# A fused attention and MLP block on one core: VectorE's score units moved to the projection banks, projections ordered by need, LN1 scaling on one engine

## The chip, the core and the metric

The kernel runs on 1 core of a Trainium2 chip. The engines of that core work side by side: TensorE (PE in the profile; PEld is its weight load), VectorE (DVE), ScalarE (ACT), GpSimd (POOL) and SyncE (SP), which here only issues DMAs. The metric is the device time of one execution in microseconds; the number given for a kernel is the median of its runs.

## The reference

One block with adaptive layer norm, on a sequence of S = 2048 tokens of width D = 640, with H = 32 heads of 20 and an MLP of width 1536. All inputs are bf16.

```
mod = silu(c) @ w_mod                      # six vectors of 640: sa, ca, ga, sb, cb, gb
h = layernorm(x) * (1 + ca) + sa
q, k, v = h @ wqkv, split in 32 heads of 20
p = softmax(q @ k.T / sqrt(20))            # 32 heads, 2048 x 2048 each
x = x + ga * ((p @ v) @ wo)
h = layernorm(x) * (1 + cb) + sb
x = x + gb * (((h @ w_gate) * (h @ w_up)) @ w_down)
```

## The kernel before

**Tiling.** Heads go in sets of four (index j, 8 sets). One set fills TensorE by tiling: scores use four row tiles of 32 rows (head s of the set at rows 32s), PV uses four column tiles. Queries go in five chunks (CHUNKS, L351): three of 512, two of 256. An *item* is one chunk and one set; there are 40, taken chunk by chunk. A *unit* is one PSUM bank of scores: one head, 128 keys by 512 queries, or two key tiles by 256 queries. Each item has 64 units in the chunks of 512 and 32 in the others.

**Two ways to take the exponential.** ScalarE takes most units: it reads two or three neighbouring banks in one instruction (L999) and writes bf16 probabilities to a ring PP of 8 slots. VectorE takes the rest, four units (a *quad*) at a time: each unit is turned into a 16-bit integer that is read as a bf16 power of two (DB0, L1026), then the quad is shifted by five constants (DSS, L1039), and PV sums all six versions (L1364). QUADS (L352) gives the quads of an item: 2, 3, 3, 1, 1 by chunk, so 320 VectorE units and 1728 ScalarE units.

**Banks.** PSUM has 8 banks. Bank 7 gathers PV. Score groups go in turn to set A (banks 0 to 2) and set B (banks 3 and 4). In chunks 1 and 2 (WIDE) set B takes bank 5 as well. A VectorE unit sits in one bank of a group of three beside two ScalarE units (L844 to L860), and the group's set becomes free when both engines have read it. What is left, pool G (banks 5 and 6, or 6 alone), serves every *round*: an accumulation of TensorE in one bank with its evacuation (class Round, L610), for LN1 transposes (hT), K, Q and V projections, modulation columns, attention output (op), LN2 transposes, gate, up and down.

**Order.** The program of every engine is a fixed list, made by a planner in Python (class Sched, L94) with assumed durations. Each engine takes the ready task of lowest priority number. TensorE (pick_pe, L1476) takes the next score group if its set is free, then PV units in batches, then a step of a round (pick_x, L1448), then filler matmuls that keep its clock up. Rounds can carry a gate: the score group from which on they may start. `late` (L923 to L939) gives gates to the K, Q and V rounds so that they spread over chunk 0; `suffix` (L1129) does the same for op, LN2 and MLP of a chunk over the stretch of the next chunk, up to the fraction GATE_F.

**The head.** Loads of x, w_mod and the weights are issued from SP's and ScalarE's queues (L548 to L587). c is loaded transposed, one element to a partition (L548), for silu (L602 to L605). LN1 (ln1, L684) has two statistics instructions a tile on VectorE, the power -1/2 on GpSimd, and the scaling xn (L701): on VectorE for token blocks 0 and 1, on GpSimd for blocks 2 and 3 (XN_POOL). Its transposes are evacuated to hT (L721) on VectorE, two in five on ScalarE (HT_ACT). Once all projections are done, the down weights are loaded over hT's place (L946) and multiplied by gb on GpSimd (L949).

**The tail.** The last chunk's op, LN2 and MLP have no exponentials beside them. Its x is loaded (L1150) once the chunk before has written its output, whose buffer it takes.

Of the kernel before, what the change touches and what calls it, by code (L numbers as in the profile page):

```python
# [12 lines left out]
SEM = 60.0  # L13
# [4 lines left out]
DMA_RATE = 260.0  # L18
# [75 lines left out]
class Sched:  # L94

    def __init__(self):
        self.tasks = []
        self.order = {k: [] for k in ("sp", "act", "pe", "dve", "pool")}
        self.all = []
        self.free_at = {k: 0.0 for k in self.order}  # L100
        self.pend = {k: [] for k in self.order}
        self.readyl = {k: [] for k in self.order}
        self.t = 0.0
        self.n = 0
        self.progress = 0
# [9 lines left out]
        self.nfill = 0  # L115
        self.hist = []
        self.left = 0
# [31 lines left out]
    def activity(self, t, area):  # L149
        self.roll(t)  # L150
        self.ham_act += area
        self.hist.append((t, area))

# [198 lines left out]
QUADS = [2, 3, 3, 1, 1]  # L352
# [21 lines left out]
def build_kernel(nc, A_x, A_wqkv, A_wo, B_x, B_w_gate, B_w_up, B_w_down, c, w_mod, out):  # L374
# [61 lines left out]
    zfill = alloc("zfill", [128, 512], BF16)  # L436
    mhalf = alloc("mhalf", [128, 4], F32)
    warm = alloc("warm", [128, 1], F32)
    qcol = alloc("qcol", [128, 1], F32)
    csb = alloc("csb", [128, KD], BF16)  # L440
# [23 lines left out]
    for (_, n) in CHUNKS:  # L464
# [20 lines left out]
    WKQ = 2 * D + 32  # L485
    r_size = max(KD * S * 2 + KD * WKQ * 2 + KD * D * 2,
                 FT * D * 2 + FT * 512 * 2 + KD * 512 * 2 + 2 * 4 * D * 2 + 2 * KD * 128 * 2)
    r_off = region(r_size)
    R1 = Sub(r_off, r_size)
    hT = R1.alloc("hT", [128, KD, S], BF16)  # L490
    wkq = R1.alloc("wkq", [128, KD, WKQ], BF16)
    wV = R1.alloc("wV", [128, KD, D], BF16)
    R2 = Sub(r_off, r_size)
    wd_sb = R2.alloc("wd", [128, FT, D], BF16)
# [44 lines left out]
    cv = c.rearrange("o (k p) -> p (o k)", p=128)  # L539
# [8 lines left out]
    def load_c(e):  # L548
        with nc.allow_non_contiguous_dma(reason="tiny transposed c load"):
            return e.dma_start(csb[:, :], cv[:, :])  # L550

    d_c = dma("act", 4096, load_c, prio=0, dur=550.0)
# [23 lines left out]
    load_w(d_wk, 0, 1, wkq, 0, "sp", 2)  # L576
    load_w(d_wq, 0, 0, wkq, D, "act", 2)
# [7 lines left out]
    load_w(d_wk, 1, 1, wkq, 0, "sp", 5.3)  # L585
    load_w(d_wq, 1, 0, wkq, D, "sp", 5.2)
# [6 lines left out]
    p_on = pool(2400, lambda e: e.memset(Vf[:, :].rearrange("p (h w) -> p h w", w=VW)[:, :, 0:1], 1.0), prio=2)  # L593
    d_pz = dve(500, lambda e: e.memset(ps[:, BPV, :], 0.0), prio=0)
    d_zf = dve(200, lambda e: e.memset(zfill[:], 1.0), prio=0.5)
    d_wz = dve(100, lambda e: e.memset(wkq[:, :, 2 * D:WKQ], 0.0), prio=0)
# [5 lines left out]
    a_ex = act(300, lambda e: e.activation(ex[:], csb[:], AFT.Exp, scale=-1.0), [d_c], prio=5)  # L602
    d_e1 = dve(70, lambda e: e.tensor_scalar(ex1[:], ex[:], 1.0, None, op0=ALU.add), [a_ex], prio=0)
    d_rc = dve(70, lambda e: e.reciprocal(rc[:], ex1[:]), [d_e1], prio=0)
    d_sc = dve(70, lambda e: e.tensor_tensor(scol[:], rc[:], csb[:], ALU.mult), [d_rc], prio=0)  # L605
    d_SC = dve(420, lambda e: e.tensor_copy(SCb[:], scol[:].unsqueeze(2).to_broadcast([128, KD, 128])), [d_sc], prio=8)

    follower = {}

    class Round:  # L610
        def __init__(self, mms, deps, after, prio, gate=0, name=""):
# [24 lines left out]
            prev = self.evac[-1].on_start  # L636

            def rel(task):
                if prev is not None:
                    prev(task)  # L640
                G.done(b["b"], task)
            self.evac[-1].on_start = rel
# [12 lines left out]
    def col_round(v, slot, prio, plus):  # L655
# [15 lines left out]
        return r  # L671

# [37 lines left out]
    def hT_rounds(tc, prio):  # L710
# [3 lines left out]
        for k in range(KD):  # L714
# [6 lines left out]
            def after(r, k=k):  # L721
                dst = hT[:, k, tc * 512:(tc + 1) * 512]
# [14 lines left out]
    proj_last = []  # L737

    def w_deps(kind, j):
        if kind == "K":  # L740
            return [d_wk[(80 * j) // 320]] + ([d_wk[1]] if j == 3 else []) + ([d_wq[0], d_wz] if j == 7 else [])
        return [d_wq[(80 * j) // 320]] + ([d_wq[1]] if j == 3 else []) + [d_wz]

    def kq_round(kind, j, tc, prio, gate=0):
        w0 = 80 * j + (0 if kind == "K" else D)
        mms = []
        for k in range(KD):
            f = [lambda e, b, k=k, s=s: e.matmul(  # L748
                ps[32 * s:32 * s + 32, b, :], wkq[:, k, w0 + DH * s:w0 + DH * s + 32], hT[:, k, tc * 512:(tc + 1) * 512],
# [26 lines left out]
        proj_last.append(r.last)  # L776

    def v_round(t, ch, prio, gate=0):
        mms = []
        for k in range(KD):  # L780
            f = quarters(320, lambda k=k: hT[:, k, t * 128:(t + 1) * 128],
# [3 lines left out]
        def after(r):  # L785
            f = lambda e: e.tensor_copy(
                Vf[:, (t * H + 16 * ch) * VW:(t * H + 16 * ch + 16) * VW].rearrange("p (h w) -> p h w", w=VW)[:, :, 1:VW],
                ps[:, r.b["b"], 0:320].rearrange("p (h w) -> p h w", w=DH))
            return [dve(ps_cost(320), f, [r.last, p_on], prio=1)]
        r = Round(mms, list(t_hT[t // 4]) + [d_wv[ch]], after, prio, gate=gate, name=f"V{t}.{ch}")  # L790
        v_ready[(t, ch)] = r.evac[0]
        proj_last.append(r.last)

# [8 lines left out]
    class Unit:  # L802
        __slots__ = ("item", "ci", "j", "s", "kts", "n", "task", "pslot", "off", "pv_ready", "is_d", "quad", "grp", "first")
# [36 lines left out]
    ap, dp = 0, 0  # L840
    quad_left = []
    while ap < NA or dp < len(dlist):
        even = len(glist) % 2 == 0
        wide = 3 if even or ap >= NA or ubuf[ap].ci in WIDE else 2  # L844
        us = ubuf[ap:ap + wide]
        d = None
        if not quad_left and dp < len(dlist):
            quad_left = dlist[dp:dp + 4]
        if wide == 3 and quad_left and due[dp] <= ap:
            two = ubuf[ap:ap + 2]  # L850
            for u in quad_left:
                if u.s not in [v.s for v in two]:
                    d, us = u, two
                    break
        if d is not None:
            d.first = len(quad_left) == 4
            quad_left.remove(d)
            dp += 1
        ap += len(us)
        glist.append((us, d, 0 if even else 3, wide))  # L860
# [6 lines left out]
    widen, narrow = set(), set()  # L867
    bw = 2
    for g in range(1, NG, 2):
        w = glist[g][3]  # L870
        if w > bw:
            widen.add(g)
        if w < bw:
            narrow.add(g)
        bw = w

    for tc in range(4):
        ln1(tc, 2.0 + tc)
        hT_rounds(tc, 10 + 20 * tc)
# [6 lines left out]
    r_sb = col_round(3, 2, 78, False)  # L886
    r_cb = col_round(4, 3, 79, True)
# [33 lines left out]
    def g0(item):  # L921
        return max(0, int(gi * item))
    late = []  # L923
    for j in range(1, NSET):
        late.append((j - 1.2, 2560, lambda p, g, j=j: kq_round("Q", j, 0, p, g)))
        for tc in range(4):
            late.append((j - 1.15 + .2 * tc, 2560, lambda p, g, j=j, tc=tc: kq_round("K", j, tc, p, g)))
    for t in range(NT):
        late.append((0.7 + 2.6 * t / NT, 1600, lambda p, g, t=t: v_round(t, 1, p, g)))
    ql = [(tc, j) for tc in range(1, 4) for j in range(NSET)]  # L930
    for i, (tc, j) in enumerate(ql):
        late.append((3.0 + 4.7 * i / len(ql), 2560, lambda p, g, j=j, tc=tc: kq_round("Q", j, tc, p, g)))
# [3 lines left out]
    for i, (dl, w, f) in enumerate(late):  # L936
        even = NSET * acc / tot
        f(100 + i, g0(max(0.0, min(dl, even))))
        acc += w  # L939

# [35 lines left out]
    for g, (us, du, b0, wide) in enumerate(glist):  # L976
# [3 lines left out]
        allu = us + ([du] if du is not None else [])  # L980
        for i, u in enumerate(allu):
# [3 lines left out]
        ts.acq = [(bset, "b", 1 if du is None else 2)]  # L985
        if g in widen:
            ts.acq.append((G, "g5", 1, 5))
        if g in narrow:
            lastw = [act_of[g - 2]] + [d_state[glist[g - 2][1].quad[0]]["p1"][glist[g - 2][1].quad[1]]
                                       for _ in range(1) if glist[g - 2][1] is not None]  # L990
            ts.on_start = lambda task, lastw=lastw: G.add(5, lastw)
        sc.left += 1
        ts.seq = -1
        score_q.append((ts, allu))
# [22 lines left out]
        if du is not None:  # L1017
            qi, x = du.quad
            st_ = d_state[qi]
            if du.first:  # L1020
                ts.acq.append((sB0, "b0", NSH))
                assert ts.on_start is None
                ts.on_start = lambda task, st_=st_: st_.__setitem__("slot", task.slots["b0"])

            def fp1(e, st_=st_, x=x, b=b0 + nu):
                return e.tensor_scalar(DB0[:, st_["slot"], x * 512:(x + 1) * 512], bank(b), EBIAS, 0.0,  # L1026
                                       op0=ALU.add, op1=ALU.max)
            tp = Task("dve", ps_cost(512), fp1, [ts], prio=0.8, name=f"P1.{qi}.{x}")
            tp.on_start = lambda task, bset=bset: bset.done(0, task)
            sc.add(tp)  # L1030
# [98 lines left out]
    def suffix(ci):  # L1129
# [18 lines left out]
        def pr():  # L1148
            return pbase + rc_[0]
        d_xc = dma("sp", 128 * ntl * D * 2, lambda e: e.dma_start(xck[:, 0:ntl, :], xv[:, t0:t0 + ntl, :]),  # L1150
                   out_prev + proj_last, prio=15, gate=max(0, gb - 20))
# [3 lines left out]
        for tl in range(ntl):  # L1155
# [17 lines left out]
            for hf in range(2):  # L1173
                bn.append(dve(ps_cost(320), lambda e, tl=tl, hf=hf: e.bn_stats(  # L1174
                    st2[:, tl, 6 * hf:6 * hf + 6], xck[:, tl, 320 * hf:320 * hf + 320]), [ev[hf]], prio=2.8))
# [425 lines left out]
```

## Time and profile before

| what | value |
|---|---|
| median of 3 runs | 927.5 us (925.35 to 927.86) |
| profiled execution | 926.16 us, with a span of 924.3 us from the first to the last instruction |
| busy in the span | PE 858.5 us, ACT 815.4 us, DVE 729.0 us, POOL 77.8 us |
| mean granted TensorE clock | 0.978 of full speed |

The profile is of one execution. Its page has the busy time of each engine, slices of the span with the busy share of each engine in tenths, and the costliest groups of instructions; a group's row has its line, engine and operation, what it writes and reads, its count, its busy time in us and the mean of one in ns, then the idle time of the engine just ahead of it and what ended that. Busy time counts overlapping neighbours once. Matmuls are pipelined, so a busy PE is not PE at its peak. In a timeline a row begins with its start and length in us, and square brackets give the idle time ahead of it.

### The profile page before, as it was taken

The page shows a single profiled execution, that of the slowest core. Times are in us where ns is not written, and L with a number is a line of the kernel's source. Part 1 is how long each engine was busy: PE and PEld are TensorE (multiplying, and loading weights), DVE is VectorE, ACT ScalarE, POOL GpSimd, SP SyncE. Part 2 cuts the span into 40 slices and gives each one's busy share as a digit, 9 for nine tenths or more (in the row PEclk, how much of TensorE's full clock was granted, in tenths as well). Part 3 has the DMA queues.
Part 4 walks back from the last instruction along what each step waited for, and adds up shares of the span by engine and source line. Part 5 has one row for each costly group of instructions (what it writes and reads, how often), then busy time and mean ns, then how long its engine had stood idle before and what let it go on. Part 6 is the DMA issues. An engine that isn't in the chain of part 4 may idle for free.

```text
span 924.3 us, 31230 instructions
## 1 busy us (share of the span) xinstructions
PE 858.5 (93%) x13925; PEld 336.2 (36%) x13938; DVE 729.0 (79%) x1333; ACT 815.4 (88%) x774; POOL 77.8 (8%) x97
## 2 busy tenths in 40 slices
PE   5769999999997889999989799999999999999968
PEld 2324333323221322323333223333344445445547
DVE  6747877777779999989889989989777866687743
ACT  1636999999997999999999999999999999999911
POOL 3823000000006300000000000000010000000000
PEclk7979999999998999999999999999999999999989
DMA  9320000000024002210030012200301225415100
GB/s 294 106 73 2 6 5 6 5 6 4 5 54 110 6 19 48 49 33 5 30 81 5 5 42 51 48 6 20 91 8 39 64 64 111 106 29 111 43 24 18
DMA packets 101197, 42.31 MB, mean 46 GB/s; under 512 B 81864, under 2 KB 101064, under 8 KB 101064
## 3 DMA queue, kind: packets, MB, share of 16 engines
q1 hardware_dynamic: 98552, 38.44, 16.7%
q8 instruction: 110, 1.80, 0.8%
q10 hardware_dynamic: 2512, 1.89, 0.7%
q14 instruction: 23, 0.19, 0.1%
HBM read 35.06 MB, written 2.62 MB: 41 GB/s over the span
## 4 chain that ended last, share of the span: by engine, by line
PE 64%; DVE 18%; ACT 10%; POOL 4%; issue 2%; DMA 2%; SPq 1%; POOLq 0%; ACTq 0%; DVEq 0%
PE ps_all L646 19%; PE ps_all L961 18%; PE ps_all L1364 17%; ACT PP L999 10%; PE ps_all L748 8%; DVE DSS L1039 6%; DVE DB L1026 5%; POOL xn L701 2%; DMA x<-in_A_x_dram 1%; DVE xck L1165 1%; DVE st L1174 1%; DMA xck<-in_A_x_dram 1%; SPq L1110 1%; DVE h2T L1196 1%; DVE OT L1091 1%
## 5 line engine op out<-in xcount | busy, mean ns | idle before, releaser
L999 ACT ACTIVATE PP<-ps_all 128x1024 bf16<-128x1024 f32 (+1 forms) x751 | 803.9, 1167 | 53.5 <-PE ps_all L961 48.3
L961 PE MATMUL ps_all<-QT,KT 32*128 32x512 bf16 (+1 forms) x2560 | 296.5, 341 | 17.9 <-ACT PP L999 11.5
L1039 DVE TENSOR_SCALAR DSS<-DB 128x2048 int16<-128x2048 int16 x400 | 274.1, 702 | 19.9 <-PE ps_all L1364 17.9
L1026 DVE TENSOR_SCALAR DB<-ps_all 128x512 int16<-128x512 f32 x320 | 216.3, 681 | 39.2 <-PE ps_all L961 37.5
L961 PEld LDWEIGHTS ps_all<-QT,KT 32*128 32x128 bf16 x2560 | 77.3, 91 | 265.8 <-ACT PP L999 181.5
L1364 PE MATMUL ps_all<-PP,Vf 128*32 128x512 bf16 (+3 forms) x2176 | 164.2, 344 | 0.4 <-DVE OT L1091 0.2
L1364 PE MATMUL ps_all<-DSS,Vf 128*32 128x512 bf16 (+3 forms) x1920 | 145.0, 346 | 6.1 <-DVE DSS L1039 5.9
L646 PE MATMUL ps_all<-h2T,stg 128*32 128x512 bf16 (+1 forms) x1960 | 127.3, 354 | 1.9 <-DVE gsb L1236 1.0
L748 PE MATMUL ps_all<-hT,wkq 128*32 128x512 bf16 x1280 | 93.2, 389 | 0.5 <-ACT hT L724 0.5
L1364 PEld LDWEIGHTS ps_all<-PP,Vf 128*32 128x32 bf16 (+1 forms) x2176 | 48.0, 94 | 78.8 <-issue 71.8
L646 PE MATMUL ps_all<-wd,hprod 128*32 128x320 bf16 x1536 | 69.7, 301 | 0.7 <-DVE hprod L1246 0.5
L1364 PEld LDWEIGHTS ps_all<-DSS,Vf 128*32 128x32 bf16 (+1 forms) x1920 | 51.9, 96 | 33.4 <-DVE DSS L1039 14.2
L646 PEld LDWEIGHTS ps_all<-h2T,stg 128*32 128x32 bf16 x1960 | 41.9, 95 | 49.0 <-issue 24.1
L1177 POOL TENSOR_SCALAR sd<-mv 128x1 f32<-128x1 f32 x16 | 4.9, 308 | 573.5 <-DVE mv L1176 573.5
L1246 DVE TENSOR_TENSOR hprod<-ps_all,gsb 128x512 bf16<-128x512 f32 (+1 forms) x60 | 34.7, 579 | 20.9 <-PE ps_all L646 20.7
L646 PEld LDWEIGHTS ps_all<-wd,hprod 128*32 128x32 bf16 x1536 | 36.1, 96 | 25.7 <-issue 11.8
L748 PEld LDWEIGHTS ps_all<-hT,wkq 128*32 128x32 bf16 x1280 | 27.1, 97 | 38.4 <-issue 21.4
L646 PE MATMUL ps_all<-wo,Ocp 128*32 128x320 bf16 x640 | 33.5, 316 | 5.7 <-DMA xck<-in_A_x_dram 4.4
L949 POOL TENSOR_TENSOR wd<-wd,gab 128x640 bf16<-128x640 bf16 x12 | 20.4, 1738 | 200.6 <-DMA wd<-in_B_w_down_dram 200.6
L761 DVE TENSOR_SCALAR QT<-ps_all,qcol 128x512 bf16<-128x512 f32 (+1 forms) x40 | 24.9, 638 | 14.4 <-PE ps_all L748 14.4
L1091 DVE STREAM_TRANSPOSE OT<-ps_all 128x512 f32<-128x512 f32 (+1 forms) x40 | 24.2, 604 | 14.7 <-PE ps_all L1364 14.7
L1364 PE MATMUL ps_all<-DB,Vf 128*32 128x512 bf16 (+3 forms) x384 | 33.7, 347 | 1.3 <-DVE OT L1091 1.0
(62 smaller groups left out, 449.9 us busy)
## 6 DMA issues: line engine op xcount, KB each, us to landing
stg<-in_B_w_gate_dram SPq DMA_DIRECT2D x49, 160.0 KB, 2.5
stg<-in_B_w_up_dram SPq DMA_DIRECT2D x49, 160.0 KB, 2.8
out_dram<-xck SPq DMA_DIRECT2D x16, 160.0 KB
wm<-in_w_mod_dram SPq DMA_DIRECT2D x3, 800.0 KB
x<-in_A_x_dram SPq DMA_DIRECT2D x6, 320.0 KB
xck<-in_A_x_dram SPq DMA_DIRECT2D x3, 640.0 KB
wd<-in_B_w_down_dram SPq DMA_DIRECT2D x1, 1920.0 KB
stx<-in_B_w_gate_dram SPq DMA_DIRECT2D x11, 160.0 KB
```

The costliest lines, as they stand in the source:

```text
L646: return lambda e, b: e.matmul(ps[32 * x:32 * x + 32, b, 0:n], lhs()[:, 32 * x:32 * x + 32], rhs(), tile_position=(0, 32 * x), start=st, s ...
L701: f = lambda e, t=t, i=i: e.tensor_scalar(xn[:, s2, i, :], x0[:, t, :], mv[:, t, 0:1], rs[:, t:t + 1], op0=ALU.subtract, op1=ALU.mult)
L748: f = [lambda e, b, k=k, s=s: e.matmul(ps[32 * s:32 * s + 32, b, :], wkq[:, k, w0 + DH * s:w0 + DH * s + 32], hT[:, k, tc * 512:(tc + 1) * ...
L761: f = lambda e, ci=ci, so=so, n=n: e.tensor_scalar(QT[ci][:, j, :], ps[:, r.b["b"], so:so + n], qcol[:, 0:1], None, op0=ALU.mult)
L949: t_wd.append(pool(1400, lambda e, f_=f_: e.tensor_tensor(wd_sb[:, f_, :], wd_sb[:, f_, :], gab[:, 1, :], ALU.mult), [d_wd] + ev_gb, prio=21))
L961: ems.append(lambda e, i=i, kt=kt: e.matmul(dstf()[:, i * u.n:(i + 1) * u.n], KT[32 * u.s:32 * u.s + 32, u.j, kt * 128:(kt + 1) * 128], QT ...
L999: return e.activation(PP[:, cellp["p"], 0:nu * 512], ps[:, b0:b0 + nu, :].rearrange("p b c -> p (b c)"), AFT.Exp, scale=ESCALE)
L1026: return e.tensor_scalar(DB0[:, st_["slot"], x * 512:(x + 1) * 512], bank(b), EBIAS, 0.0, op0=ALU.add, op1=ALU.max)
L1039: return e.tensor_scalar(DSS[:, cell["s"], :], DB0[:, st_["slot"], :], float(SHIFTS[jj]), None, op0=ALU.add)
L1091: t1 = Task("dve", n * 1.1 + 70, lambda e: e.transpose(OT[:, 0:n], ps[:, BPV, 0:n]), [], prio=0.0, name=f"T1.{it}")
L1246: f = lambda e: e.tensor_tensor(hprod[:, fc, 0:n], ps[:, r.b["b"], 0:n], gsb[:, gs, 0:n], ALU.mult)
L1364: ems.append(lambda e, i=i, kt=kt, stt=stt, stp=stp: e.matmul(ps[32 * s:32 * s + mc, BPV, 0:u.n], Vf[:, (kt * H + 4 * u.j + s) * VW:(kt * ...
```

## The change

1. *VectorE units.* Score groups hold ScalarE units only, 3 and 2 in turn, in banks 0 to 2 and 3 to 4, in all chunks. When TensorE is about to issue a group, `d_attach` appends up to two VectorE units in a free row tile, into banks of pool G, where they stay until VectorE has read them. If they fall behind, they get a pass of their own, and rounds leave them a bank (`d_wants`). Item 0 of chunks 1 and 2 has two quads in place of three: 312 VectorE units, 1736 ScalarE units.
2. *Order of projections.* Every round of the head and of chunk 0 gets a priority from the item in which it is needed (`need`), the gates follow, and the Q rounds of later chunks come last. wk and wq become two tiles, hT four.
3. *LN.* XN_POOL is empty (all LN1 scalings on VectorE), HT_ACT keeps ScalarE's part for block 0 only, LN2 has priority 0.7 on VectorE in place of 2.8. GATE_F falls.
4. *c* is loaded as five rows, transposed by TensorE and copied by VectorE.
5. PV batches: PVMIN, PVMAX, PVCAP from 8, 12, 24 to 10, 10, 16. Score groups are issued twice where TensorE has had little to do and ScalarE is busy for long (DUP_MIN). The filler uses the identity.

```
-QUADS = [2, 3, 3, 1, 1]
+QUADS = [2, (2, 3, 3, 3, 3, 3, 3, 3), (2, 3, 3, 3, 3, 3, 3, 3), 1, 1]
-WIDE = (1, 2)
-PVMIN, PVMAX, PVCAP = 8, 12, 24
-GATE_F = [0.98, 0.98, 0.95, 0.8, 1.0]
+PVMIN, PVMAX, PVCAP = 10, 10, 16
+GATE_F = [0.7, 0.7, 0.6, 0.5, 1.0]
+DUP_MIN = 4200.0
-XN_POOL = (2, 3)
-HT_ACT = ((1, 3), (1, 3), (1, 3), (1, 3))
+XN_POOL = ()
+LN2P = 0.7
+HT_L = 0.12
+V_L = 0.5
+LATE_A = 0.8
+LATE_L = 1.6
+LATEQ = ()
+HT_ACT = ((1, 3), (), (), ())
...
-    d_c = dma("act", 4096, load_c, prio=0, dur=550.0)
+    d_c = dma("act", 1280, lambda e: e.dma_start(c5[:, :], cv[:, :]), prio=0, dur=550.0)
...
+    r_c = Round([(60.0, lambda e, b: e.transpose(bankh(b)[:, 0:KD], c5[:, :], ident[0:KD, 0:KD]))], [d_c, p_id], c_evac,
+                0, name="cT")
...
+        us = ubuf[ap:ap + (3 if even else 2)]
...
+    def need(x):
+        return 13 + 10 * x
     for tc in range(4):
         ln1(tc, 2.0 + tc)
-        hT_rounds(tc, 10 + 20 * tc)
+        hT_rounds(tc, 10 if tc == 0 else need(tc / 4 - HT_L))
...
-    r_sb = col_round(3, 2, 78, False)
-    r_cb = col_round(4, 3, 79, True)
+    r_sb = col_round(3, 2, need(1.6), False)
+    r_cb = col_round(4, 3, need(1.65), True)
...
-    ev_ga = gab_round(2, 0, 90)
-    ev_gb = gab_round(5, 1, 91)
+    ev_ga = gab_round(2, 0, need(1.7))
+    ev_gb = gab_round(5, 1, need(1.75))
...
-            kq_round("K", 0, tc, 13 + 20 * tc)
+            kq_round("K", 0, tc, need(tc / 4))
         for t in range(4 * tc, 4 * tc + 4):
-            v_round(t, 0, 14 + 20 * tc)
+            v_round(t, 0, need(t / 16 + V_L))
...
-        late.append((j - 1.2, 2560, lambda p, g, j=j: kq_round("Q", j, 0, p, g)))
+        late.append((j - .05, 2560, lambda p, g, j=j: kq_round("Q", j, 0, p, g)))
...
-        late.append((3.0 + 4.7 * i / len(ql), 2560, lambda p, g, j=j, tc=tc: kq_round("Q", j, tc, p, g)))
+        late.append((7.9 + .001 * i, 2560, lambda p, g, j=j, tc=tc: kq_round("Q", j, tc, p, g)))
...
-        even = NSET * acc / tot
-        f(100 + i, g0(max(0.0, min(dl, even))))
+        even = LATE_A + (NSET - LATE_A) * acc / tot
+        f(need(nd), int(gi * max(0.0, min(nd - LATE_L, even))))
```

The new function, cut to its core, and its call in pick_pe:

```
+    def d_attach(ts, t, pos, rows, limit, relax):
...
+            for u in dst["left"]:
+                if (u.s not in rows or relax) and all(d.done is not None and d.done + SEM <= t for d in unit_score_deps(u)):
+                    pick = u
+                    break
...
+            ga = G.avail()
+            if ga is None or ga[0] > t:
+                break
...
+            b, rel = G.take(ga[1], 1)
...
+            ts.deps = ts.deps + unit_score_deps(pick) + rel
+            ts.emits = ts.emits + unit_score_emits(pick, lambda b=b: bank(b))
...
+                d_attach(ts, t, apos[g], rows, 2, False)
+                dur = 216.0 * max(rows.values()) * clk()
...
+                if sc.recent(t) + area < DUP_MIN and sc.free_at["act"] > start + 2 * dur + 100:
+                    ts.emits = ts.emits + ts.emits
```

More of the change, by code (lines that the diff above doesn't have):

```diff
@@ L776, in kq_round @@
         proj_last.append(r.last)
+        if kind == "K" or tc not in LATEQ:
+            proj_early.append(r.last)
     def v_round(t, ch, prio, gate=0):
@@ L839, in build_kernel @@
     NA = len(ubuf)
-    ap, dp = 0, 0
-    quad_left = []
-    while ap < NA or dp < len(dlist):
+    ap = 0
+    apos = []
+    while ap < NA:
         even = len(glist) % 2 == 0
[L844 to L858, printed above, removed]
+        us = ubuf[ap:ap + (3 if even else 2)]
+        apos.append(ap)
         ap += len(us)
-        glist.append((us, d, 0 if even else 3, wide))
+        glist.append((us, 0 if even else 3))
     NG = len(glist)
@@ L979, in build_kernel @@
         deps = []
[L980 to L981 removed]
+        for i, u in enumerate(us):
             deps += unit_score_deps(u)
@@ L1458, in pick_x @@
                 cand = task
+                if task.acq and d_wants() and len(G.free) < 2:
+                    cand = None
+                    continue
                 if task.acq and not sc.acquire(task, t):
@@ L1495, in pick_pe @@
             if all(a.done is not None for a in la):
-                for b in range(3 + bw):
+                for b in range(5):
                     G.add(b, la)
@@ L1500, in pick_pe @@
         if sc.recent(t) < FILL_MIN and len(pP.free) >= RINGLOW and pick_x(t):
+            return True
+        if XFIRST and len(pP.free) >= XFIRST and pick_x(t):
+            just_s[0] = False
             return True
```

254 lines of the change are left out of this document (151 added, 103 removed).

## The prediction

> **What bounds the kernel now.** The page comes first, then ScalarE's groups by form, then the busy time by stage, with the stages cut where ScalarE's work changes character, then the chain of waits.
>
> ```profile
> ACT  1636999999997999999999999999999999999911
> ```
>
> ```profile
> L999 ACT ACTIVATE PP<-ps_all 128x1024 bf16<-128x1024 f32 x525 | 514.3, 1039 | 37.4 <-PE ps_all L961 33.4 <-PE ps_all L1364 1.7
> L999 ACT ACTIVATE PP<-ps_all 128x1536 bf16<-128x1536 f32 x226 | 323.6, 1464 | 16.1 <-PE ps_all L961 14.9
> ```
>
> The slices show three parts: a ragged head of four slices, a long plateau on which ScalarE is full, and a tail of two slices without it. The plateau is exponentials (L999). Both forms together are busy 803.9 us on the page; the means would give 525 x 1.039 + 226 x 1.464 = 876.3 us, so neighbours overlap by 72.4 / 751 = 0.096 us. A two-bank exponential really costs 0.943 us, a three-bank one 1.368 us.
>
> ```profile
> core 0: us, PE busy (x) PEld busy (x) DVE busy (x) ACT busy (x) POOL busy (x), PEclk, DMA share, GB/s
> ...
> 24.18:92.04 67.86, 54.96 (x878) 24.71 (x881) 42.11 (x88) 38.09 (x39) 33.28 (x29) 0.87 0.17 56
> 92.04:271.00 178.96, 178.96 (x2494) 56.17 (x2490) 134.09 (x225) 174.99 (x171) 0.00 (x0) 1.00 0.02 5
> 271.00:306.00 35.00, 26.55 (x295) 7.46 (x285) 31.52 (x45) 29.91 (x28) 18.53 (x11) 0.90 0.42 107
> 306.00:482.00 176.00, 166.83 (x2353) 55.42 (x2355) 161.67 (x283) 173.11 (x155) 5.83 (x9) 1.00 0.15 35
> 482.00:690.00 208.00, 198.16 (x2920) 69.09 (x2923) 188.94 (x337) 205.78 (x187) 6.20 (x14) 1.00 0.13 31
> 690.00:880.20 190.20, 186.61 (x4022) 92.48 (x4029) 139.47 (x271) 185.82 (x182) 3.28 (x6) 1.00 0.32 69
> 880.20:924.30 44.10, 32.43 (x837) 24.28 (x831) 15.73 (x40) 4.47 (x12) 1.56 (x4) 0.92 0.07 22
> ```
>
> From 92 to 880 us ScalarE idles only 3.97 + 5.09 + 2.89 + 2.22 + 4.38 = 18.6 us. From its first exponential at 24.18 to 92.04 it idles 67.86 - 38.09 = 29.8 us, and a few more microseconds there are hT evacuations, not exponentials. So there is little to win on the plateau, and up to 30 us in the head. The head's idle time has names:
>
> ```profile
> 44.24 0.79 ACT L724 ACTIVATE hT<-ps_all,mcol 128x512 bf16<-128x512 bf16 x1
> 57.91 1.94 ACT L999 ACTIVATE PP<-ps_all 128x1024 bf16<-128x1024 f32 x2 [12.88 <-PE ps_all L961]
> ...
> 82.06 4.76 ACT L999 ACTIVATE PP<-ps_all 128x1024 bf16<-128x1024 f32 x5 [5.47 <-PE ps_all L961]
> ```
>
> ```profile
> 27.59 2.53 POOL xn L701
> ...
> 50.49 2.52 POOL xn L701
> ...
> 76.39 1.47 PE ps_all L646 x40
> ...
> 79.43 2.29 PE ps_all L748 x40
> ```
>
> The chain of waits runs through eight LN1 scalings on GpSimd, one after another, from 27.59 to 53.01 us. The K projection of the last two token blocks cannot start before them, and ScalarE's order is fixed, so it stands still for 12.88 us. The 5.47 us belong to the order of the projections: the gab rounds (L646, 76.39 to 79.43) go ahead of the K rounds of item 1 that ScalarE is waiting for.
>
> **The change part by part.**
>
> *LN1 scaling to VectorE (XN_POOL empty), hT evacuations of blocks 1 to 3 to VectorE (HT_ACT), projections by need.*
>
> ```profile
> L701 POOL TENSOR_SCALAR xn<-x,mv,rs 128x640 bf16<-128x640 bf16 x8 | 20.2, 2529 | 0.2
> ...
> L727 DVE TENSOR_SCALAR hT<-ps_all,mcol 128x512 bf16<-128x512 bf16 x12 | 6.4, 537 | 14.4 <-PE ps_all L717 14.3
> ...
> L701 DVE TENSOR_SCALAR xn<-x,mv,rs 128x640 bf16<-128x640 bf16 x8 | 3.5, 442 | 1.3 <-POOL rs L699 1.2
> ```
>
> Off GpSimd go 8 x 2.53 = 20.2 us; onto VectorE come 8 x 0.44 = 3.5 us and 6 x 0.54 = 3.2 us; off ScalarE go six hT evacuations of the 0.79 us shown above. What is late next? To bring the kernel to the state it has at 92.04, VectorE needs 42.1 + 3.5 + 3.2 = 48.8 us after 24.18; TensorE needs its 54.96, less the gab rounds (76.39 to 79.43, about 3 us) and the two small modulation rounds (about 1.5 us) that "need" puts off, so 50.4 us; ScalarE needs about 34 us (38.09 less the hT work, 6 x 0.79 before overlap). The latest is TensorE, and it is the row I take: 67.9 to 50.4, **-17.5 us**. The far ends: -28 if TensorE's later share (V rounds for late keys, at a granted clock of 0.87) can be pushed behind ScalarE's needs, and -8 if VectorE, now carrying statistics, scaling, hT, K and V evacuations in one queue, makes the next block wait nearly as GpSimd did. Queued behind each scaling on VectorE, which waits for GpSimd's power (L699), are the evacuations that free the projection banks.
>
> *c as rows.*
>
> ```profile
> 1.23 8.22 DMA x<-in_A_x_dram
> ```
>
> ```profile
> csb<-in_c_dram ACTq DMA_DIRECT2D x1, 1.2 KB, 4.9
> ```
>
> ```profile
> 13.05 0.82 PE L660 MATMUL ps_all<-scol,wm 128*128 128x1 bf16 x25 [2.11 <-DMA wm<-in_w_mod_dram]
> ...
> 15.76 0.53 DVE L727 TENSOR_SCALAR hT<-ps_all,mcol 128x512 bf16<-128x512 bf16 x1
> ```
>
> The 1.2 KB of c takes 4.9 us to land and stands ahead of half of the first x block on ScalarE's DMA queue. As five rows it should be out of the way early; the added transpose and copy (one TensorE and one VectorE instruction of under 0.3 us each) lie beside the wait for w_mod. With x earlier, the next limit is w_mod, whose second half lets its round run from 13.05 to 13.87, after which mcol is one small copy, some 0.2 us, away. So the first hT evacuation moves from 15.76 to about 14.1: **-1.7 us**, between 0 (bandwidth, not order, held x up) and -4.
>
> *VectorE units through the projection banks.* Today such a unit takes one of the three banks of a score group, which ScalarE shares; afterwards every group carries 3 or 2 ScalarE units in turn, and up to two VectorE units ride along in banks 5 and 6. By the code chunk 0 has 512 units of which 64 are VectorE's: 512 / 2.5 = 205 groups become 448 / 2.5 = 179. The price of a group is that of one 512-column pass:
>
> ```profile
> 220.06 0.39 PE L961 MATMUL ps_all<-QT,KT 32*128 32x512 bf16 x2
> 220.37 0.61 PE L748 MATMUL ps_all<-hT,wkq 128*32 128x512 bf16 x8
> 220.92 0.39 PE L961 MATMUL ps_all<-QT,KT 32*128 32x512 bf16 x3
> ```
>
> Two and three row tiles take the same 0.39 us, and the next work starts 0.31 us on. That a fourth costs nothing is not in the trace; the step from two to three is the nearest row, and I take 0 (at worst 0.31 us more for each of 64 in chunk 0, 20 us of TensorE). So 26 x 0.31 = 8 us of TensorE go in chunk 0, some 7 of them after the head; the 4.5 us put off come in. From 92 to 271 TensorE is busy in all of 178.96 us, so it and not ScalarE sets this stretch: **-2.5 us**, between 0 and -5. ScalarE's own work in chunk 0 falls from 166 x 0.943 + 38 x 1.368 = 208.5 to 448 / 5 x 2.311 = 207.1 us, which fits beneath. In chunks 1 and 2 it goes from 96 x 0.943 + 75 x 1.368 = 193.1 to 420 / 5 x 2.311 = 194.1 us each (the first item gives four units back to ScalarE), in the last two from 83 x 0.943 + 19 x 1.368 = 104.3 to 103.5 each: **+0.4 us** together.
>
> The 5.09 us of idle time from 271 to 306 are a VectorE jam: GpSimd multiplies the down weights by gb there, and a shift takes up to 1.87 us.
>
> ```profile
> L1039 DVE TENSOR_SCALAR DSS<-DB 128x2048 int16<-128x2048 int16 x400 | 274.1, 702 | 19.9 <-PE ps_all L1364 17.9
> ```
>
> ```profile
> 286.36 18.53 POOL L949 TENSOR_TENSOR wd<-wd,gab 128x640 bf16<-128x640 bf16 x11 [200.59 <-DMA wd<-in_B_w_down_dram]
> 286.44 1.87 DVE L1039 TENSOR_SCALAR DSS<-DB 128x2048 int16<-128x2048 int16 x1
> ```
>
> The multiplication stays. But the item beneath it has two quads instead of three, and a late VectorE no longer holds a bank of ScalarE's: **-3 us**, between 0 and -5. The Trainium skill ("SBUF — State Buffer", section "Who interferes with whom") says that GpSimd and a VectorE instruction in a two-port mode lock each other out of a shared port for a whole instruction; the 1.87 against 0.70 us agrees. By it the shifts stay slow as long as the multiplication lasts, and this term would be 0.
>
> *Tail (LN2P, GATE_F).*
>
> ```profile
> 882.19 0.46 DVE xck L1266
> ...
> 885.36 0.71 SPq L1110
> ...
> 886.17 2.91 DMA xck<-in_A_x_dram
> ...
> 893.15 0.40 DVE st L1174
> ```
>
> ```profile
> Ocp<-OcT SPq DMA_DIRECT2D x6, 16.0 KB, 1.7
> ```
>
> The last chunk's x is fetched at 886.17, since its buffer is held by the previous chunk's output; with the MLP of that chunk let in from half its old distance (GATE_F 0.8 to 0.5) the fetch goes long before, and the attention output's own copies are what ends last: issued until 886.07, 1.7 us to landing, 887.8 in place of 889.08, so -1.3. The previous chunk's last addition (0.46 us at 882.19) no longer stands ahead of the transpose that these copies wait for: -0.5. With LN2 first on VectorE two statistics of 0.40 us no longer pile up behind the last addition: -0.8. Together **-2.6 us**, from 0 to -4.
>
> Sum: -17.5 - 1.7 - 2.5 + 0.4 - 3.0 - 2.6 = -26.9 us. The profiled execution took 926.16 us beside a span of 924.30, and what lies around the span stays, so 899.3; the median of the runs is 1.3 us above it, so **900 us**.
>
> **The rivals.**
>
> *VectorE takes GpSimd's place (909 us).* For it: 48.8 us of VectorE work against TensorE's 50.4, in one queue with waits for GpSimd in it. Against: from 45 to 54 us VectorE idles 8.69 us in one piece. Price: the head gives -8 instead of -17.5.
>
> ```profile
> 53.77 0.54 DVE L727 TENSOR_SCALAR hT<-ps_all,mcol 128x512 bf16<-128x512 bf16 x1 [8.69 <-PE ps_all L717]
> ```
>
> *ScalarE alone bounds the head (889 us).* The "need" order puts off all that isn't ScalarE's, and the debt is paid where TensorE has room, after 271. Price: -28 instead of -17.5.
>
> *The banks run out (about 940 us, slower).* Banks 5 and 6 serve every projection and MLP round, one after another. An evacuation in chunk 0 follows the last every 3.1 us:
>
> ```profile
> 223.33 0.71 DVE L761 TENSOR_SCALAR QT<-ps_all,qcol 128x512 bf16<-128x512 f32 x1
> ...
> 226.46 0.68 DVE L757 CAST KT<-ps_all 128x512 bf16<-128x512 f32 x1
> ```
>
> ```profile
> L1026 DVE TENSOR_SCALAR DB<-ps_all 128x512 int16<-128x512 f32 x320 | 216.3, 681 | 39.2 <-PE ps_all L961 37.5
> ```
>
> Some 58 rounds of 3.1 us fill 179 us. If a VectorE unit holds the second bank at each round's end, the next round waits for its 0.68 us: 64 x 0.68 = 43 us in chunk 0, 926 - 27 + 43 = 942. It turns the result slower from 40 of those 64 on (27 / 0.68). Against it: the matmuls of a waiting round are replaced by PV work, and TensorE loses nothing while there is some. The Trainium skill ("TensorEngine Tiling (Array Packing)", section "PSUM Bottleneck") speaks against the change in this sense: tiling speeds up TensorE and not the evacuation of its banks. The trace neither bears it out nor excludes it, since no VectorE unit uses these banks yet.
>
> **How the numbers follow.** Forecast 0.55, VectorE in GpSimd's place 0.18, ScalarE alone 0.17, banks 0.10. A measurement of this kernel can tell about 0.3%, 3 us. The range 886 to 914 holds the first three with the bounds of the small terms and leaves out the banks and some of the edges. Faster: 0.90, from the first three with a little of the fourth's weak form; within 0.3%: 0.02; slower: 0.08.
>
> **What would show it.** Right: no GpSimd scaling in the chain; ScalarE's gap of 12.9 us below 5 and none of 5 us near item 1; the idle total before the plateau down by some 17 us; about 695 exponentials busy some 802 us; score passes with four tiles still 0.39 us; the last x fetch before the last exponential. Wrong: score passes longer than 0.5 us, plateau idle above 25 us, or projection rounds in chunk 0 further apart than 3.5 us with TensorE waiting for VectorE.

## The result and the profile after

The kernel after takes 898.1 us (896.6 to 901.9, 4 runs) against 927.7 us (median of 4 runs of the kernel before): a ratio of 0.9688, 95% interval 0.9651 to 0.9726. The forecast was 900. Its profiled execution is the slowest of the four, 901.88 us with a span of 899.9, so the rows below explain 24 us and the medians 30.

First, ScalarE's exponentials alone (L999 before, L1000 after), in windows that end where a chunk's last exponential ends: chunk 0 to chunk 4, then the tail. The columns are window and length in us, busy time and count of exponentials, granted clock, DMA share and GB/s. Of before:

```profile
24.18:274.08 249.90, 212.36 (x206) 0.97 0.07 20
274.08:473.73 199.65, 191.69 (x172) 0.98 0.18 45
473.73:667.08 193.35, 191.13 (x172) 1.00 0.14 34
667.08:775.68 108.60, 105.48 (x103) 1.00 0.20 46
775.68:880.11 104.43, 103.27 (x102) 1.00 0.39 83
880.11:924.26 44.15, 0.00 (x0) 0.92 0.07 22
```

And of after:

```profile
23.17:251.47 228.30, 205.69 (x180) 0.99 0.07 21
251.47:457.31 205.84, 192.17 (x168) 0.96 0.18 44
457.31:650.71 193.40, 190.91 (x169) 0.99 0.14 33
650.71:754.49 103.78, 103.15 (x91) 1.00 0.22 51
754.49:856.66 102.17, 101.89 (x91) 1.00 0.38 83
856.66:899.95 43.29, 0.00 (x0) 0.96 0.09 26
```

Read them side by side: the first exponential comes 1.0 us sooner, chunk 0 is 21.6 us shorter, chunk 1 is 6.2 us *longer*, chunk 2 the same, chunks 3 and 4 together 7.1 us shorter, the tail 0.9 us shorter. That sums to -24.3 us. The busy times have a second change in them: all exponentials together are busy for 793.8 us in place of 803.9, 6.7 us less in chunk 0, 2.3 in chunk 3 and 1.4 in chunk 4. Beside the gaps of 12.88 and 5.47 us of before stands ScalarE's timeline in the head of after:

```profile
42.62 6.95 ACT L1000 ACTIVATE PP<-ps_all 128x1024 bf16<-128x1024 f32 x6 [5.21 <-PE ps_all L969]
...
58.30 10.49 ACT L1000 ACTIVATE PP<-ps_all 128x1536 bf16<-128x1536 f32 x9 [7.38 <-PE ps_all L969]
...
89.08 27.32 ACT L1000 ACTIVATE PP<-ps_all 128x1536 bf16<-128x1536 f32 x24 [4.40 <-PE ps_all L969]
```

The one large gap has become two middling ones with much the same sum, 12.6 us, and the gap near item 1 is only 1.1 us shorter. But by the end of the second of them (58.3 us) ScalarE has read 40 banks of scores, where before, at the end of its one gap (57.9 us), it had read 24. In the chain of waits of after no GpSimd scaling is left; VectorE's queue now stands where it stood:

```profile
29.33 0.35 DVE xn L720
29.80 0.36 DVE st L711
30.16 0.59 DVE KT L777
30.75 0.40 DVE Vf L808
31.15 0.35 DVE xn L720
```

### The profile page after: what moved, and what is told of

The parts are those of the page before. It is cut to its first block, busy times and chain, and to the rows that moved or that the text cites. A ratio compares the mean times of both kernels' runs of the same rounds, so it can differ in the third digit from the quotient of the medians.

```text
span 899.9 us, 31137 instructions
## 1 busy us (share of the span) xinstructions
PE 851.7 (95%) x13944; PEld 338.3 (38%) x13944; DVE 727.2 (81%) x1330; ACT 801.4 (89%) x712; POOL 56.8 (6%) x89
## 4 chain that ended last, share of the span: by engine, by line
PE 49%; ACT 32%; DVE 12%; issue 4%; POOL 1%; DMA 1%; SPq 0%; ACTq 0%; POOLq 0%; DVEq 0%
ACT PP L1000 32%; PE ps_all L653 15%; PE ps_all L969 14%; PE ps_all L1362 13%; PE ps_all L768 5%; DVE DSS L1038 2%; DVE DB L1024 2%; DVE xn L1180 1%; DMA x<-in_A_x_dram 1%; DVE st L711 1%; DVE st L1173 1%; DVE xck L1164 1%; POOL rs L1178 1%; DVE hT L746 1%; DVE xn L720 0%
## 5 line engine op out<-in xcount | busy, mean ns | idle before, releaser
L1000 ACT ACTIVATE PP<-ps_all 128x1536 bf16<-128x1536 f32 (+1 forms) x695 | 793.8, 1278 | 46.1 <-PE ps_all L969 42.3
L969 PE MATMUL ps_all<-QT,KT 32*128 32x512 bf16 (+1 forms) x2623 | 292.3, 343 | 14.5 <-ACT PP L1000 8.8
L1038 DVE TENSOR_SCALAR DSS<-DB 128x2048 int16<-128x2048 int16 x390 | 264.8, 695 | 29.5 <-PE ps_all L1362 27.1
L1024 DVE TENSOR_SCALAR DB<-ps_all 128x512 int16<-128x512 f32 x312 | 211.4, 681 | 42.8 <-PE ps_all L969 41.4
L1362 PE MATMUL ps_all<-DSS,Vf 128*32 128x512 bf16 (+2 forms) x1880 | 145.1, 349 | 0.5 <-DVE DSS L1038 0.2
L653 PE MATMUL ps_all<-h2T,stg 128*32 128x512 bf16 (+1 forms) x1960 | 130.6, 355 | 1.4 <-DVE DB L1024 0.9
L768 PE MATMUL ps_all<-hT,wk 128*32 128x512 bf16 x640 | 48.0, 395 | 0.5 <-DVE gab L910 0.4
L768 PE MATMUL ps_all<-hT,wq 128*32 128x512 bf16 x640 | 46.3, 385 | 1.9 <-DVE DB L1024 1.3
L653 PEld LDWEIGHTS ps_all<-wd,hprod 128*32 128x32 bf16 x1536 | 35.9, 96 | 27.8 <-issue 16.4
L1235 DVE CAST gsb<-ps_all 128x512 bf16<-128x512 f32 (+1 forms) x48 | 29.6, 616 | 8.8 <-PE ps_all L653 8.6
L1362 PE MATMUL ps_all<-DB,Vf 128*32 128x512 bf16 (+2 forms) x376 | 35.0, 349 | 0.0
```

The lines of the kernel that those rows point to most:

```text
L653: return lambda e, b: e.matmul(ps[32 * x:32 * x + 32, b, 0:n], lhs()[:, 32 * x:32 * x + 32], rhs(), tile_position=(0, 32 * x), start=st, s ...
L768: f = [lambda e, b, k=k, s=s: e.matmul(ps[32 * s:32 * s + 32, b, :], wx[:, k, w0 + DH * s:w0 + DH * s + 32], hT[tc][:, k, :], tile_positio ...
L969: ems.append(lambda e, i=i, kt=kt: e.matmul(dstf()[:, i * u.n:(i + 1) * u.n], KT[32 * u.s:32 * u.s + 32, u.j, kt * 128:(kt + 1) * 128], QT ...
L1000: return e.activation(PP[:, cellp["p"], 0:nu * 512], ps[:, b0:b0 + nu, :].rearrange("p b c -> p (b c)"), AFT.Exp, scale=ESCALE)
L1038: return e.tensor_scalar(DSS[:, cell["s"], :], DB0[:, st_["slot"], :], float(SHIFTS[jj]), None, op0=ALU.add)
L1235: f = lambda e: e.tensor_copy(gsb[:, gs, 0:n], ps[:, r.b["b"], 0:n])
```

## The experiments

Names that begin with "Before" or "After" say which kernel was edited. Every ratio is to the kernel before; differences in us are between medians.

**Before with the scalings on VectorE.**

```
-XN_POOL = (2, 3)
+XN_POOL = ()
```

> The kernel before with XN_POOL empty and nothing else. Head theory (GpSimd's scalings hold up blocks 2 and 3): the 12.9 us gap of ScalarE shrinks to under 4, the 5.5 us gap behind the gab rounds stays; 914 to 918 us. Rival, VectorE takes GpSimd's place: the gap only changes its releaser, 924 to 929 us. Rival, the banks bring the gain: also 924 to 929 us.

Measured: 914.1 us, ratio 0.987 (0.9849 to 0.9891). One constant brings 13 of the 30 us. ScalarE's timeline of this run has a gap of 2.75 us where there were 12.88, and the 5.47 unchanged:

```profile
44.42 5.17 ACT L999 ACTIVATE PP<-ps_all 128x1024 bf16<-128x1024 f32 x5 [2.75 <-PE ps_all L961]
...
68.07 4.76 ACT L999 ACTIVATE PP<-ps_all 128x1024 bf16<-128x1024 f32 x5 [5.47 <-PE ps_all L961]
```

So VectorE does not take GpSimd's place in full, and the 5.47 us, which the prediction puts down to the order of projections, do not hang on the scalings.

**Before with all of the head's edits.** In addition to the above:

```
-HT_ACT = ((1, 3), (1, 3), (1, 3), (1, 3))
+HT_ACT = ((1, 3), (), (), ())
...
-        hT_rounds(tc, 10 + 20 * tc)
+        hT_rounds(tc, 10 if tc == 0 else need(tc / 4 - .12))
...
+        even = .8 + (NSET - .8) * acc / tot
+        f(need(dl), g0(max(0.0, min(dl - 1.6, even))))
```

with the other `need` lines of the change.

> The kernel before with all of the head's edits (XN_POOL empty, HT_ACT for block 0 only, rounds ordered by need), banks, LN2, gates, c and PV batches as before. Head theory: ScalarE's idle time and hT work ahead of the plateau fall from 34 us to about 20; 908 to 914 us, and what is left to the kernel after (898) is 10 to 15 us. Rival, the banks bring the gain: 918 us or more.

Measured: 905.8 us, ratio 0.978 (0.9755 to 0.9805), a little better than expected. Its first two windows:

```profile
24.38:252.10 227.72, 211.30 (x206) 1.00 0.07 21
252.10:452.91 200.81, 192.34 (x172) 1.00 0.19 45
```

Chunk 0 takes 227.7 us here and 228.3 in after: the head's edits alone account for the whole gain of chunk 0. What the rest of the change adds there cancels: ScalarE spends 37.5 us of chunk 0 without an exponential before, 16.4 here and 22.6 in after, while the exponentials are busy for 212.4, 211.3 and 205.7 us. After saves 5.6 us of ScalarE's work against this run and loses 6.2 us in waiting.

**After with the scalings back on GpSimd.**

```
-XN_POOL = ()
+XN_POOL = (2, 3)
```

> The kernel after with the scalings of blocks 2 and 3 back on GpSimd (XN_POOL = (2, 3)). Head theory: a gap of ScalarE of 10 us or more between 40 and 60 us; 907 to 912 us. Rival, VectorE takes GpSimd's place: within 3 us of 898.

Measured: 915.7 us, ratio 0.9868 (0.983 to 0.9907): 17.6 us lost, more than the 9 to 14 expected. Chunk 0 takes 244.6 us. The idle time does not come as one gap of 10 us but as five of 2.7 to 7.4 us that end between 40 and 76 us; that the new order has other rounds to put between is the likely reason, not shown. The sign is the head theory's, the form is not.

**After without the head, LN2 and gate edits: the banks alone.** Undone are XN_POOL, HT_ACT, the order, LN2P, GATE_F and the PV batches; left are the VectorE units in banks 5 and 6, QUADS, the doubled groups, c as rows and the split tiles of wk, wq and hT.

```
-XN_POOL = ()
+XN_POOL = (2, 3)
...
-LN2P = 0.7
+LN2P = 2.8
...
-GATE_F = [0.7, 0.7, 0.6, 0.5, 1.0]
+GATE_F = [0.98, 0.98, 0.95, 0.8, 1.0]
```

> The kernel after with the scalings, HT_ACT, order of rounds, LN2 priority, GATE_F and PV batches of before: what is left is VectorE's units in the projection banks, the smaller QUADS, the doubled score groups and c as rows. Head theory: head as before, plateau a little denser; 918 to 925 us. Rival, the banks bring the gain: 912 us or less. Rival, the banks run out: 935 us or more.

Measured: 923.3 us, ratio 0.9963 (0.9946 to 0.9981), in the expected place, but for a reason that no theory had. Its last three windows:

```profile
664.34:767.43 103.09, 102.54 (x91) 1.00 0.18 43
767.43:870.09 102.66, 102.29 (x91) 1.00 0.40 87
870.09:922.93 52.84, 0.21 (x1) 0.94 0.13 34
```

Chunks 3 and 4 are 7.3 us shorter than before, the whole of what after has gained there. But the tail is 52.6 us (the last window still has 0.2 us of an exponential), 8.5 longer than before. The chain of waits of this run says what stands in it:

```profile
868.94 4.79 DMA stg<-in_B_w_up_dram
...
875.50 6.73 PE ps_all L653 x192
882.26 0.50 DVE xck L1265
882.77 1.80 DMA out_dram<-xck
884.59 2.95 DMA xck<-in_A_x_dram
```

After the last exponential the previous chunk's MLP is not done: its last gate and up weights are still to land, and 192 down matmuls follow, before the last chunk can even fetch its x. What the exponentials saved was lost again to MLP work left over.

**After with LN2 last on VectorE.**

```
-LN2P = 0.7
+LN2P = 2.8
```

> The kernel after with LN2P = 2.8, LN2 last on VectorE again. Theory L (LN2 first, with its scalings slowed by GpSimd's multiplication, pushes the shifts back and costs the 6 us that chunk 1 is longer than before): chunk 1 falls from 206 to about 200 us, 892 to 895 us, the tail 0.5 to 1 us longer. Rival G (the multiplication alone does it): chunk 1 stays at 204 to 207 us, within 3 us of 898. Rival E (the earlier gates do it): the same.

Measured: 907.0 us, ratio 0.9775 (0.976 to 0.9789): 9 us *slower*. Theory L had the first half right and fell by the second:

```profile
250.16:451.52 201.36, 191.45 (x168) 0.97 0.18 43
...
852.96:904.93 51.97, 0.25 (x1) 0.97 0.14 37
```

Chunk 1 is 4.5 us shorter, as expected. The tail, from the last exponential on 51.7 us, is 8.4 us longer, not 0.5 to 1, again with 192 down matmuls of the previous chunk in it (858.86 to 865.59). LN2 first costs time in chunk 1 and is what gets the MLPs nearly done before the exponentials end.

**After with the old gates.**

```
-GATE_F = [0.7, 0.7, 0.6, 0.5, 1.0]
+GATE_F = [0.98, 0.98, 0.95, 0.8, 1.0]
```

> The kernel after with GATE_F of before (0.98, 0.98, 0.95, 0.8). Rival E (earlier gates crowd the start of chunk 1): chunk 1 falls to about 200 us, 892 to 895 us. Theories L and G: chunk 1 as in after, 898 within 3 us. The prediction's tail term says that the fetch of the last x comes after the last exponential again and the tail is 1 to 2 us longer; the trace of after, where it came after it too, says that the tail does not change.

Measured: 898.6 us, ratio 0.9679 (0.9661 to 0.9696): no difference to after. Tail 43.2 us, the same. Chunk 1 is at 203.0 us, between the theories; the early fetch after (below), whose order in chunk 1 is that of after, has 204.3, so these windows differ by 1.6 us from one execution to another. The gates do not decide. That TensorE and VectorE have no time for the MLP sooner is the likely reason, not shown.

**After without the multiplication of the down weights.** This leaves the factor gb out of the output.

```
-        t_wd.append(pool(1400, lambda e, f_=f_: e.tensor_tensor(wd_sb[:, f_, :], wd_sb[:, f_, :], gab[:, 1, :],
-                                                                ALU.mult), [d_wd] + ev_gb, prio=21))
+        t_wd = [d_wd] + ev_gb
```

> The kernel after without the multiplication of the down weights by gb on GpSimd; that factor is left out of the output. Rival G (port between GpSimd and VectorE): chunk 1 falls to 197 us or less, 887 to 891 us, shifts at 0.7 us throughout. Theory L: about half of it, 893 to 896 us, since LN2 then has fast scalings but still stands ahead of the shifts.

Measured: 892.5 us, ratio 0.9611 (0.9587 to 0.9636): 5.6 us less than after. The shifts of this run (L1037, VectorE, from 280 to 345 us, minimum / median / maximum in ns) and those of after from 292 to 319 us (L1038):

```profile
L1037 DVE TENSOR_SCALAR DSS<-DB x34: 630/683/696, 279.4 to 342.9; 128x2048 int16<-128x2048 int16 x34
```

```profile
L1038 DVE TENSOR_SCALAR DSS<-DB x10: 627/834/1481, 291.7 to 315.2; 128x2048 int16<-128x2048 int16 x10
```

No shift is longer than 0.7 us without the multiplication, as rival G says. Chunk 1 falls to 199.7 us, from 205.8 in after and 203.0 with the old gates: the multiplication is worth 3 to 6 us of it, 5.6 by the medians, between the two expectations. The granted clock in chunk 1 is 0.98 here and 0.96 in after, so some of this may be the clock's.

**After with c transposed in the load.** As before, one element to a partition, without the transpose on TensorE.

```
-    d_c = dma("act", 1280, lambda e: e.dma_start(c5[:, :], cv[:, :]), prio=0, dur=550.0)
+    d_c = dma("act", 4096, load_c, prio=0, dur=550.0)
```

> The kernel after with c loaded one element to a partition, as before, and no transpose on TensorE. Prediction's term: the second half of the first x block lands 2 us later, the first hT evacuation 1.7 us later; 899 to 901 us. Rival (another load sets the first hT): first hT within 0.5 us of after, 897 to 899 us.

Measured: 899.1 us, ratio 0.969 (0.967 to 0.971), not to be told from after. The first hT on ScalarE starts at 16.00 us here and at 14.47 in after, so c as rows does bring 1.5 us there. The first exponential starts 0.8 us sooner (23.16 against 23.93), and chunk 0 gives that back (226.4 us here, 228.3 in after). The prediction's step holds at the first hT; the total is the rival's.

**After with the last x fetched early.** The last chunk takes the other half of the buffer.

```
+        xck = xck_all[:, 2:4, :] if tail else xck_all[:, 0:4, :]
...
-                   out_prev + proj_early, prio=15, gate=max(0, gb - 20))
+                   (out_two if tail else out_prev) + proj_early, prio=15, gate=max(0, gb - 20))
```

> The kernel after with the last chunk's x in the other half of its buffer, so that its fetch waits for the output of the chunk before the previous one and not of the previous one. The prediction's tail term: the fetch leaves the chain, the attention output's copies end last, the tail shrinks by 1.3 us to about 42; 896 to 898 us. Rival (the copies or the rest of the previous chunk's MLP end as late anyway): the first op matmul starts as long after the last exponential as in after, no change.

Measured: 896.0 us, ratio 0.9681 (0.966 to 0.9703). The medians alone do not separate it from after. The tail does, 40.0 us against 43.3; with the late fetch it was 43.0 to 43.7 in three more kernels (old gates, no multiplication, c transposed). The chain of waits, of after and then of this run:

```profile
862.30 0.71 SPq L1109
...
863.11 2.86 DMA xck<-in_A_x_dram
...
866.02 0.89 PE ps_all L653 x20
```

```profile
857.73 0.74 SPq L1109
858.51 1.83 DMA Ocp<-OcT
860.38 0.89 PE ps_all L653 x20
```

The fetch is gone from the chain and the attention output's copies end last. From the last exponential to the first op matmul it takes 7.5 us (852.85 to 860.38) in place of 9.4 (856.66 to 866.02). The rest of the 3.3 us goes with a clock of 1.00 in this tail against 0.96, whose cause was not tried.

**After with LN2 last for chunk 0 alone.**

```
     def suffix(ci):
+        LN2P = 2.8 if ci == 0 else 0.7
```

> The kernel after with LN2 last on VectorE for chunk 0 alone (it runs beside GpSimd's multiplication), first for the others. If the price in chunk 1 and the debt in the tail are separate: chunk 1 about 201 us, tail 43 us, 893 to 896 us. Rival (a late start of any chunk's MLP is carried to the end): chunk 1 about 201 us, tail 48 us or more, 900 us or more.

Measured: 903.1 us, ratio 0.9742 (0.9727 to 0.9757). The rival was right, but for a tail of 47.1 us in place of its 48: chunk 1 takes 201.4 us, and what it saves is lost again, 3.6 us in chunks 2 to 4 and 3.8 in the tail. A late start of chunk 0's MLP, four chunks ahead, is still paid at the end.

**After with the multiplications spread.**

```
+    for f_, t_ in enumerate(t_wd):
+        d_ = act_of[gstart[1] + 20 + 5 * f_]
+        t_.deps.append(d_)
```

> The kernel after with the twelve multiplications of the down weights spread over chunk 1: each also waits for an exponential, the first for the 20th of the chunk, then every fifth. Theory G (the burst of multiplications blocks VectorE at the wrong time): chunk 1 falls from 206 to about 200 us, 892 to 895 us, like the kernel without them (892.5). Rival (the same lock time, only cut up): chunk 1 stays at 204 us or more, 896 to 899 us.

Measured: 907.1 us, ratio 0.9776 (0.9746 to 0.9806): 9 us slower than after, worse than either theory, though its six runs lie far apart (901.0 to 910.0). Chunk 1 takes 208.3 us and the tail 45.3. Shifts stand beside a multiplication from 290 to 349 us, and in after only from 293 to 318; and the down matmuls, which need all twelve, can start only later. Which of the two costs more was not taken apart.

**Early fetch, with the gab rounds one item later.**

```
-    ev_ga = gab_round(2, 0, need(1.7))
-    ev_gb = gab_round(5, 1, need(1.75))
+    ev_ga = gab_round(2, 0, need(2.7))
+    ev_gb = gab_round(5, 1, need(2.75))
```

> The kernel with the early fetch of the last x, and the four gab rounds put off by one item (need 2.7 and 2.75 in place of 1.7 and 1.75), with them GpSimd's multiplication of wo. If the 4.4 us gap of ScalarE at 85 to 89 us comes from gab evacuations that hold the banks while GpSimd's multiplication slows the shifts beside them, and later items have K rounds in hand: no gap over 2 us from 75 to 95 us, chunk 0 at 225 us or less, 892 to 894 us. Rival (the jam moves along with the rounds): a gap of 3 us or more one item later, 895 to 897 us.

Measured: 898.3 us, ratio 0.97 (0.9676 to 0.9724). The gap is gone, as the first theory says (1.23 us is the longest between 71 and 102 us), and chunk 0 takes 225.6 us, 2.7 less than with the early fetch alone. But chunk 2 is 3.1 and chunk 4 3.2 us longer, and the total is 898.3 against 896.0, outside both expectations. The time freed ahead was given back later; why was not tried.

## Why the prediction was right, point by point

The number was right, 900 against 898, and the first rank of causes too: the LN1 scalings and the order of the head. Some of the terms were not, and they cancelled: in the profiled execution chunk 1 came out 9 us worse than its -3, chunks 3 and 4 together 5.5 us better than the -1.6 that was counted for them, the tail 1.7 us worse. That the sum comes so near is in that part luck.

- **Head, first exponential and chunk 0 (-17.5, -1.7 and -2.5): right in the sum and in the first cause, not in the split.** Measured -1.0 and -21.6. Shown by the kernel before with the head's edits alone, whose chunk 0 is 22.2 us shorter, and by undoing the scalings in after. So the head's edits were worth more than 17.5, and the -2.5 for fewer score groups is not borne out: after's chunk 0 is no shorter than that. The first hT evacuation moved to 14.12 us, as forecast (14.1), but the first exponential came 1.0 us sooner and not 1.7. "The idle total before the plateau down by some 17 us" did not come: it was 29.8 us before, and the head's edits alone leave 15.5 (the first row, ScalarE alone), but after has 22.1 (the second row, all engines; ScalarE's 46.73 is the fourth busy time):

```profile
24.38:92.04 67.66, 52.13 (x52) 1.00 0.18 57
```

```profile
23.17:92.04 68.87, 64.79 (x1009) 28.03 (x1008) 58.22 (x119) 46.73 (x41) 14.44 (x21) 0.95 0.18 57
```

  The other 14 of chunk 0's 21.6 us are some 4 us of hT work that left ScalarE, 3.5 us of idle time behind 92 us, and 6.7 us of the exponentials' own time. What holds the head now is not TensorE alone, as the row I took said: the chain of waits is mostly VectorE's from 20 to 39 us and mostly TensorE's from 39 to 60, with gaps of ScalarE of 3.7, 5.2, 7.4 and 4.4 us left. "ScalarE's gap of 12.9 us below 5 and none of 5 us near item 1" was wrong in its first half: there are two gaps above 5.
- **ScalarE's own work (-1.4 in chunk 0, and the +0.4): mis-sized.** I expected some 802 us of exponentials. Their number came out (695), their time did not: 793.8 us, 10.1 less than before. The step that failed is the price of one, 0.943 and 1.368 us: these are averages of before, over exponentials that follow each other at once and others that wait. Those that wait for nothing start 0.92 and 1.33 us apart in its trace; behind a wait nothing overlaps, and one of two banks takes 1.02 us. In before 131 of 751 start behind a gap, in after 60 of 695.
- **The jam of chunk 1 (-3): wrong in sign.** Chunk 1 became 6.2 us longer in the profiled execution, and 3 to 5 us with the old gates and the early fetch. Two steps failed. The first is "a late VectorE no longer holds a bank of ScalarE's": its units now hold banks that rounds and other VectorE units wait for, and in TensorE's one queue the next score group waits behind them. In after's timeline of TensorE a round waits for VectorE's evacuation (first row) and a score pass for its reading of a unit (last row):

```profile
303.32 0.73 PE L653 MATMUL ps_all<-wo,Ocp 128*32 128x320 bf16 x16 [0.99 <-DVE xck L1164]
303.98 0.39 PE L969 MATMUL ps_all<-QT,KT 32*128 32x512 bf16 x2
305.72 0.39 PE L969 MATMUL ps_all<-QT,KT 32*128 32x512 bf16 x1 [1.35 <-DVE DB L1024]
```

  So no gain came of the banks. But they do not by themselves make the chunk longer either. In the banks alone it takes

```profile
272.95:471.57 198.62, 191.10 (x168) 0.98 0.19 46
```

  and 201.4 us in after with LN2 last, against 199.7 to 202.2 in the three kernels with the old banks. The second step is LN2 first, whose price in chunk 1 the sum put at nothing: beside the multiplication the scalings of LN2 take up to 1.51 us in after, and 0.45 without it.

```profile
L1180 DVE TENSOR_SCALAR xn<-xck,mv,rs x4: 445/1206/1508, 292.4 to 315.9; 128x640 bf16<-128x640 bf16 x4
```

  Undoing LN2 first shortens chunk 1 by 1.6 to 4.5 us, leaving out the multiplication by 3 to 6; the two overlap. After with the scalings back on GpSimd has both and takes 200.7 us there, so how they meet in time matters too; that stays open. The Trainium skill's rule for the shared port ("SBUF — State Buffer", "Who interferes with whom") spoke for no gain here. Without the multiplication no shift exceeds 0.696 us, which agrees with it.
- **Chunks 3 and 4 (part of +0.4): far too small.** I counted instructions and found 0.8 us each; measured were 4.8 and 2.3. By the windows above, 2.3 and 1.4 of that are busy time of the exponentials, 2.5 and 0.9 idle time between them, which the sum left as it was. The runs show that it belongs to the banks part of the change; which of its edits brings it (the banks, the doubled groups) was not taken apart. That a group no longer waits for VectorE's reading, and that a three-bank exponential in every pair gives TensorE longer to refill the other set, is argued and not shown.
- **Fourth row tile at no cost: right.** In after four tiles take 0.40 us, two take 0.39:

```profile
77.17 0.40 PE L969 MATMUL ps_all<-QT,KT 32*128 32x512 bf16 x4
...
78.32 0.39 PE L969 MATMUL ps_all<-QT,KT 32*128 32x512 bf16 x2
```

- **Tail (-2.6): wrong.** Measured -0.9. The step that failed is "with the MLP of that chunk let in from half its old distance the fetch goes long before": it goes at 863.11, 6.5 us after the last exponential, and the old gates give the same tail. Nor did the previous chunk's addition leave the chain (-0.5): it stands there for 0.43 us at 858.66. The mechanism of the fetch itself was right, as the other buffer shows. LN2 first was put down at 0.8 us; undoing it costs 9.
- **The rival of the banks: refuted as a slowdown, right as a mechanism.** No 43 us appeared. But with the new banks and LN2 last, the MLP falls behind and the tail is 8 to 9 us longer, and LN2 first makes up for it. I had it deciding in chunk 0, and it shows at the end.

## What to carry to other kernels

When two engines are near full, look for what is left undone when the bounding engine stops: an edit can shorten several stages and lose it all in the tail, and an edit that lengthens one stage can pay for itself there. Price a move off a shared buffer by whoever now waits for the buffer it moves to. A gap in the head that is one slow engine in the chain of waits is the safest gain; here one constant brought 13 of 30 us.

## What the runs showed of the hardware

The first exponential of kernels with the same head came at 21.7, 22.2, 22.5 and 23.2 us (without the multiplication, with the old gates, with the early fetch, and after). The start of the head, where the loads are, alone differs by 1.5 us from one execution to another, so chunk lengths are the better measure for what lies behind it.

On GpSimd one multiplication of 128 x 640 takes 1.39 us at best and up to 1.95 us with VectorE's shifts beside it (in after); the shifts' time grows from 0.68 us to as much as 1.48 us in after and 1.87 before.
